# An attention decode kernel: x and bias loads issued after an early square root, and the last values load cut in four instead of three

## The chip, the cores, the metric

One core of one Trainium2 chip. The metric is the device time of one execution in microseconds (us), the median of several. Executions of one kernel mostly agree within about 0.3%. Each run also has its mean *granted clock*: the share of full speed that PE's clock was given, averaged over the execution.

## The reference

Two branches over the same layer-normed x (2 rows of 448) are added to x: attention of 16 heads over the last 4096 positions of a cache with 8 kv heads of 256, and a dense block with a mish activation.

```python
W = min(4096, max(256, Sk // 4))                        # 4096 of 32768 positions
q = (x @ wq)                                            # 2 x 4096
k, v = k_cache[:, :, Sk - W:, :], v_cache[:, :, Sk - W:, :]
p = softmax(einsum("bhqd,bhkd->bhqk", q, k) * Dh ** -0.5)
attn = einsum("bhqk,bhkd->bhqd", p, v) @ wo
h = x @ w1 + b1
dense = (h * tanh(softplus(h))) @ w2
out = x0 + attn + dense                                 # x = layernorm(x0) above
```

Of the 77.66 MB that are read, 67.1 are k and v: 8 heads of 4.19 MB each, twice. Each is read once, so the kernel is a stream with arithmetic beside it.

## The kernel before

All large loads are issued from SP, in the order in which they are used. Only x and the bias are issued from ACT. The beginning:

```python
    x_bf = consts.tile([Bsz, D], BF16)
    nc.scalar.dma_start(out=x_bf[:, :], in_=A_x.flatten_outer_dims())
    b1_sb = consts.tile([1, F], BF16)
    nc.scalar.dma_start(out=b1_sb[:, :], in_=B_b1.rearrange("(o f) -> o f", o=1))
    # ... cut
    for lo, hi in ((0, SC), (SC, NS)):
        nc.sync.dma_start(out=wq_sb[:, lo:hi, :], in_=wq_in[:, lo:hi, :])
    make_identity(nc, ident[:])
    # ... cut
    eps_t = consts.tile([Bsz, 1], FP32)
    nc.vector.memset(eps_t[:], 1e-5)
    stats = consts.tile([Bsz, nc.vector.BN_STATS_DIM], FP32)
    nc.vector.bn_stats(out=stats[:], in_=x_bf[:])
    # ... bn_aggr
    nc.scalar.activation(out=rstd[:], in_=mv[:, 1:2], func=ACT.Sqrt, bias=eps_t[:], scale=1.0)
```

From there one chain leads over xn, its transposes and xs to q (`q_ps`, 28 matmuls with wq) and its transpose, and q is needed for the first scores. The loop over the kv heads, and its end:

```python
    for i in range(Hkv + 1):
        if i + 1 < Hkv:
            load_k(i + 1, (0, T) if i + 1 < Hkv - 1 else (0, T // 2, T))
        if i < Hkv:
            load_v(i, (0, T) if i < Hkv - 1 else (0, T // 2, 7 * T // 8, T))
            load_wo(i, parts=1 if i < Hkv - 1 else 2)
            # ... four pieces of: turn (DVE transpose of k), scores (PE), exp (ACT), turn_p (DVE)
        else:
            close(i - 2)
            carry()              # running sum to the last accumulator: DVE copy, 8 products
        # ... dense block at i == 0
        if i >= 1:
            values(i - 1)        # 32 wide products; the last NFIX = 2 heads: values_fixed,
                                 # 128 small products, in the order of the positions t
        if i == Hkv:
            close(i - 1)         # oT, then 16 products with wo into psA, then out
```

A head's 4096 positions lie as T = 64 on each of 64 partitions per batch row, so the cuts (0, 32, 56, 64) give pieces of 32, 24 and 8 positions, and `values_fixed` makes two products a position: 64, 48 and 16.

The softmax here doesn't subtract the row's maximum and nothing guards it: scores larger than these inputs give would overflow.

## Time and profile before

| | before |
|---|---|
| time, three runs | 190.18 us median (189.81 to 190.29) |
| span of the profiled execution | 188.0 us |
| DMA | 77.66 MB read, 413 GB/s over the span, one queue busy 97.0% |
| PE, DVE, ACT, GpSimd busy | 77%, 57%, 23%, 9% |

Read it from the DMA row: nothing else is busy all the time. The busy slices, the start and the end of the timeline are in the prediction. What is told as a *landing* is from the trace's records of the completions of each of the 16 engines; a load has landed with the last of them.

### The profile page before, as it was taken

Reading aid. Unit: us, or ns where it says so; the run is one execution under the profiler, and the core shown is the slowest. Engines: PE = TensorE matmul, PEld = TensorE weight load, DVE = VectorE, ACT = ScalarE, POOL = GpSimd, SP = SyncE. Lnnn points to the kernel's source line nnn. Section 1 sums busy time; section 2 is a strip of 40 time slices with the busy share of each in tenths; the row PEclk is TensorE's granted clock in tenths of the full one; section 3 lists DMA queues with packets and bytes.
Section 4 is the critical chain, followed back from the end, with each engine's and each line's share of the span. In section 5 each row is a group of like instructions: output and inputs, shape, how many; then the busy total and the mean of one; then the engine's idle time right before and its main releaser. Section 6 shows DMA issues by size and latency. Waiting matters only on the chain.

```text
span 188.0 us, 2346 instructions
## 1 busy us (share of the span) xinstructions
PE 145.5 (77%) x909; PEld 67.0 (36%) x909; DVE 106.8 (57%) x142; ACT 42.5 (23%) x142; POOL 16.5 (9%) x74
## 2 busy tenths in 40 slices
PE   0395089914989988976997599958996689988983
PEld 0131033811334433432442234313442234434662
DVE  6405397049671976079804991099506993977211
ACT  3005015200062124212331223012421242125101
POOL 7000600300003000300030003000030000000000
PEclk9999558855799999997899999975999999999755
DMA  6999899999999999999999999999999899999990
GB/s 220 421 469 446 380 433 442 439 443 439 432 446 418 420 412 421 448 439 386 472 443 441 397 425 446 425 439 422 436 436 439 380 439 429 453 443 387 424 388 35
DMA packets 5652, 77.81 MB, mean 414 GB/s; under 512 B 517, under 2 KB 2569, under 8 KB 2954
## 3 DMA queue, kind: packets, MB, share of 16 engines
q1 hardware_dynamic: 5636, 77.66, 97.0%
q8 instruction: 7, 0.11, 0.2%
q14 instruction: 3, 0.02, 0.0%
q10 hardware_dynamic: 6, 0.01, 0.0%
HBM read 77.67 MB, written 0.00 MB: 413 GB/s over the span
## 4 chain that ended last, share of the span: by engine, by line
DMA 60%; DVE 19%; PE 16%; SPq 2%; ACT 1%; issue 1%; ACTq 0%; DVEq 0%
DMA k<-in_A_k_cache_dram 50%; DVE kt L386 14%; DMA v<-in_A_v_cache_dram 10%; PE o L457 7%; PE sc L398 4%; DVE pT L424 3%; PE psE L210 3%; PE q L507 1%; SPq L362 1%; ACT p L412 1%; SPq L114 0%; PE psA L227 0%; DVE oT L471 0%; PE q L488 0%; SPq L295 0%
## 5 line engine op out<-in xcount | busy, mean ns | idle before, releaser
L386 DVE STREAM_TRANSPOSE kt<-k 128x2048 f32<-128x2048 f32 x32 | 73.1, 2288 | 49.7 <-DMA k<-in_A_k_cache_dram 49.7
L398 PE MATMUL sc<-kt,qdiag 128*128 128x512 bf16 x256 | 63.9, 401 | 17.2 <-DVE kt L386 17.2
L412 ACT ACTIVATE p<-sc,off 128x256 bf16<-128x256 f32 x64 | 33.0, 545 | 73.3 <-PE sc L398 72.6
L398 PEld LDWEIGHTS <-qdiag 128*128 128x128 bf16 x256 | 24.4, 101 | 56.5 <-issue 23.2
L457 PE MATMUL o<-v,pT 128*8 128x512 bf16 x192 | 42.5, 379 | 0.0
L457 PEld LDWEIGHTS <-pT 128*8 128x8 bf16 x192 | 17.2, 92 | 22.4
L424 DVE STREAM_TRANSPOSE pT<-p 128x512 bf16<-128x512 bf16 x32 | 21.7, 677 | 6.1 <-ACT p L412 6.0
L279 POOL COPY qdiag<-qt 32x16 bf16<-32x16 bf16 x64 | 13.0, 249 | 120.9 <-PE sc L398 104.8
L210 PE MATMUL psE<-wo,oT 128*2 128x448 bf16 x28 | 8.6, 444 | 7.2 <-DVE oT L471 7.2
L412 ACT ACTIVATION_READ_ACCUMULATOR p<-sc,off 128x1 f32 x64 | 11.8, 184 | 0.0
L465 ACT COPY o_sb<-o 8x512 f32<-8x512 f32 x6 | 3.5, 575 | 36.3 <-PE o L457 36.3
L210 PE MATMUL psE<-v,act_bf 128*2 128x448 bf16 x14 | 5.2, 567 | 6.5 <-DVE act_bf L344 6.5
L259 PE MATMUL q_ps<-v,xq 128*128 128x512 bf16 x28 | 8.0, 455 | 2.9 <-DMA v<-in_A_wq_dram 2.9
L507 PE MATMUL q<-pT,v 128*128 128x4 bf16 x256 | 7.2, 168 | 0.2 <-DMA v<-in_A_v_cache_dram 0.2
L507 PEld LDWEIGHTS <-v 128*128 128x128 bf16 x256 | 7.3, 102 | 0.3 <-DMA v<-in_A_v_cache_dram 0.3
L269 DVE CAST q_sb<-q_ps 128x512 bf16<-128x512 f32 x2 | 1.3, 687 | 8.6 <-PE q_ps L259 8.6
L259 PEld LDWEIGHTS <-xq 128*128 128x128 bf16 x28 | 3.1, 112 | 7.7 <-issue 3.5
L210 PEld LDWEIGHTS <-oT 128*2 128x2 bf16 x28 | 2.0, 91 | 10.2 <-DVE oT L471 7.8
L210 PEld LDWEIGHTS <-act_bf 128*2 128x2 bf16 x14 | 1.6, 121 | 9.5 <-DVE act_bf L344 6.5
L488 PEld LDWEIGHTS q<-ident_f,o_sb 8*128 8x128 f32 x24 | 3.3, 207 | 3.0 <-issue 3.0
L180 PE MATMUL xnT_ps<-ident,xn_bf 2*128 2x2 bf16 x7 | 0.5, 166 | 4.7 <-DVE xn_bf L138 4.7
L269 ACT CAST q_sb<-q_ps 128x512 bf16<-128x512 f32 x2 | 1.1, 588 | 12.9 <-PE q_ps L259 12.9
(59 smaller groups left out, 46.0 us busy)
## 6 DMA issues: line engine op xcount, KB each, us to landing
k<-in_A_k_cache_dram SPq DMA_DIRECT2D x7, 4096.0 KB, 29.4
v<-in_A_v_cache_dram SPq DMA_DIRECT2D x7, 4096.0 KB, 29.0
k<-in_A_k_cache_dram SPq DMA_DIRECT2D x2, 2048.0 KB, 24.5
v<-in_B_w_dram SPq DMA_DIRECT2D x2, 1568.0 KB, 24.8
wo<-in_A_wo_dram SPq DMA_DIRECT2D x7, 448.0 KB, 29.7
v<-in_A_wq_dram SPq DMA_DIRECT2D x1, 2048.0 KB, 7.7
v<-in_A_v_cache_dram SPq DMA_DIRECT2D x1, 2048.0 KB, 15.4
v<-in_A_wq_dram SPq DMA_DIRECT2D x1, 1536.0 KB, 10.8
```

What stands on the lines that cost most here:

```text
L210: nc.tensor.matmul(psE[:], lhsT=lhsT, rhs=w, start=start, stop=stop, skip_group_check=True)
L259: nc.tensor.matmul(ps[u][:], lhsT=xq[:, s, :, :].rearrange("p j k -> p (j k)"), rhs=wq_sb[:, s, u * N5 : (u + 1) * N5], start=(s == 0), st ...
L269: copy(out=q_sb[:, u * N5 : (u + 1) * N5], in_=ps[u][:])
L279: nc.gpsimd.tensor_copy(out=tv[rows, :, e, j * Q : (j + 1) * Q : HS].rearrange("p n (b h) -> p n b h", b=Bsz), in_=qv[rows, :, h0 : h0 + r ...
L386: nc.vector.transpose(out=kt[:].bitcast(FP32), in_=k[:, half * TH * Dh : (half + 1) * TH * Dh].bitcast(FP32),)
L398: nc.tensor.matmul(psc[:], lhsT=qdiag[i % NW][:, n * NE + e, :], rhs=ktv[:, n, e, :, :], start=(n == 0 and e == 0), stop=(n == NB - 1 and ...
L412: nc.scalar.activation(out=pv[:, b, :, :], in_=sv[:, b, :, :], func=ACT.Exp, scale=scale, bias=off[:, b : b + 1], accum_out=state["rs", i] ...
L424: nc.vector.transpose(out=pT[:], in_=p_t.pop(s)[:])
L457: nc.tensor.matmul(po[:], lhsT=pT_t[i * NH + piece][:, uh * NP * Q : (uh + 1) * NP * Q : HS], rhs=v[:, u * NP : (u + 1) * NP, :].rearrange ...
L465: nc.scalar.copy(out=o_sb[:], in_=po[:])
L488: nc.tensor.transpose(pqv[:, u, c, :], ov[:, u, c, :], ident_f[0:NR, 0:NR])
L507: nc.tensor.matmul(po[:, c, :], lhsT=vv[:, t, c, :], rhs=pTv[:, th, 0:Q:HS], start=(t == 0 and c == 0), stop=(t == T - 1), skip_group_chec ...
```

## The change

Its intent: have ACT fetch the square root's table at the very start by a dummy root, so that the table needn't be fetched when the norm wants it, and let PE start sooner on the last values by cutting their load finer.

```diff
+    eps_t = consts.tile([Bsz, 1], FP32)
+    nc.vector.memset(eps_t[:], 1e-5)
+    root = consts.tile([Bsz, 1], FP32)
+    nc.scalar.activation(out=root[:], in_=eps_t[:], func=ACT.Sqrt)
     x_bf = consts.tile([Bsz, D], BF16)
     nc.scalar.dma_start(out=x_bf[:, :], in_=A_x.flatten_outer_dims())
     ... cut
-    eps_t = consts.tile([Bsz, 1], FP32)
-    nc.vector.memset(eps_t[:], 1e-5)
     ... cut
-            load_v(i, (0, T) if i < Hkv - 1 else (0, T // 2, 7 * T // 8, T))
+            load_v(i, (0, T) if i < Hkv - 1 else (0, T // 2, 13 * T // 16, 15 * T // 16, T))
```

## The prediction

> **What bounds the kernel now.** I read the busy slices first, to see which resource is never idle; then the queue table and the chain of waits; then the timeline of the first 25 us and the last 5 us, where the two edits lie; last the packet and landing records of the transfers there.
>
> ```profile
> DMA  6999899999999999999999999999999899999990
> GB/s 220 421 469 446 380 433 442 439 443 439 432 446 418 420 412 421 448 439 386 472 443 441 397 425 446 425 439 422 436 436 439 380 439 429 453 443 387 424 388 35
> q1 hardware_dynamic: 5636, 77.66, 97.0%
> DMA 60%; DVE 19%; PE 16%; SPq 2%; ACT 1%; issue 1%; ACTq 0%; DVEq 0%
> ```
>
> Between the first and the last slice the DMA engines are busy everywhere: 77.66 MB in a 188.0 us span, 97.0% of it on the one SP queue. The chain names DMA for 60%; its stretches on DVE and PE lie over a queue that is still full. For instance the load of v that is issued at 49.99 us finds the third k load, issued at 31.76, still queued (it landed at 59 to 61 by the landing records); and the last v loads are issued at 163.26 while earlier ones land until 173.9. So about 10 us of transfers lie queued at each of these issues, and a compute stage that slips by less than that starves nothing. The time is then: when the stream starts (first wq row at 1.75 us by the packet records), 77.66 MB at its rate, and the tail after the last byte.
>
> The start, from the timeline:
>
> ```profile
> 0.73 0.55 ACTq L100 DMA_DIRECT2D x_bf<-in_A_x_dram  x1
> 1.31 0.23 ACTq L102 DMA_DIRECT2D b_sb<-in_B_b_dram  x1
> 1.58 1.28 ACT L129 ACT_TABLE_LOAD   x1 [1.58 <-PEq L595]
> 2.06 0.61 DVE L125 BATCH_NORM_STATS2 stats<-x_bf 2x6 f32<-2x448 bf16 x1
> 2.92 0.29 ACT L129 ACTIVATE rstd<-mv,eps_t 2x1 f32<-2x1 f32 x1
> 8.46 8.01 PE L259 MATMUL q_ps<-v,xq 128*128 128x512 bf16 x28 [2.85 <-DMA v<-in_A_wq_dram]
> 21.75 4.50 DVE L386 STREAM_TRANSPOSE kt<-k 128x2048 f32<-128x2048 f32 x2 [3.25 <-DMA k<-in_A_k_cache_dram]
> 24.11 2.29 PE L398 MATMUL sc<-kt,qdiag 128*128 128x512 bf16 x5 [7.65 <-DVE kt L386]
> 40.19 2.31 DVE L386 STREAM_TRANSPOSE kt<-k 128x2048 f32<-128x2048 f32 x1 [7.86 <-DMA k<-in_A_k_cache_dram]
> ```
>
> The table load already lies beside the x load and its statistics: it ends at 2.86, and mv is ready at 2.88 (2.71 + 0.17). The idle times in brackets are the slack: q_ps waited for wq, the first turn 3.25 us for k, and the turn at 40.19 another 7.86 us for the second k load.
>
> The end:
>
> ```profile
> 180.34 1.85 PE L507 MATMUL q<-pT,v 128*128 128x4 bf16 x64
> 182.40 1.87 PE L507 MATMUL q<-pT,v 128*128 128x4 bf16 x64 [0.22 <-DMA v<-in_A_v_cache_dram]
> 184.53 0.58 PE L227 MATMUL psA<-wo,oT 128*2 128x112 bf16 x16 [0.26 <-DVE oT L471]
> ```
>
> Here 64 products of v's first piece run, PE waits 0.22 us for the second, then 64 more run without a gap. By the landing records the last engine's share of v's second piece lands at 182.36, of its third at 183.58, of wo's first half at 184.16, of wo's second half at 184.72. The product with wo's second half is the last 8 of the 16 matmuls at 184.53: at 0.036 us each (0.58/16) it starts at 184.82, only 0.10 us after its data. That is the fact that decides the second edit.
>
> **What the Trainium skill says.** "ScalarE: Activation LUTs", What ACT_TABLE_LOAD costs: about 1283 ns for the load plus a drain. The trace agrees on the load (1.28 us); no separate drain stands in it, as the square root starts 0.06 us after the load. "DMA: Bandwidth & Descriptors", Issuing engines are not separate DMA queues: a load issued from ACT runs on the same 16 engines as one from SP and interleaves with it. The same page, Queues, rings and completion order: an engine serves its queues in turn, a packet at a time. The trace shows what a late comer pays: x was issued at 0.73, its first packet ran at 1.66, 0.93 after the issue and 0.09 before the first wq row. The bias was issued at 1.31, so by the same 0.93 it should have run at 2.24; its one packet ran at 5.43, its completion packet at 6.18, and it landed at 6.49. It sat 3.2 us behind some five wq rows (0.61 us each for 16 KB), and its completion behind one more. That is harmless now, as the bias is first read at 34.05.
>
> **The change part by part.**
>
> 1. Root ahead of the loads. Removed: nothing; the kernel still loads two tables, square root and exp. Added: one ACTIVATE of 2x1 (0.29 us, as rstd's). Moved: the table load to about 0.73, ending at 2.0; the root to about 2.05; the issue of x to between 2.05 and 2.35 (whether ACT waits for the root to end I don't know), against 0.73. x's packets then reach the engines 0.93 later, at 3.0 to 3.3, with wq rows queued ahead, and I let them pay what the bias paid: 3.2 us to the packet, so 6.2 to 6.5, about 0.75 to the completion packet, 0.3 to the landing. x lands at about 7.3 instead of 2.04: 5.3 us later. rstd gains 0.05 us at most from the table being there.
>
> 2. What that does downstream. From x's statistics at 2.06 to the first weight load of q at 7.30 is one chain on DVE, ACT and PE, 5.24 us, all behind x in program order. Shifted by 5.3 it ends at 12.6. wq's second part has landed by 12.03, so q_ps now waits for xq. The 28 matmuls take 8.01 again: they end at 20.6 instead of 16.47, 4.15 later (1.15 was slack). The copies and q's transpose end at 22.65 instead of 18.5. The first turn of k stands behind it on DVE: 22.65 instead of 21.75, 0.9 later. The GpSimd copies, 20.28 + 4.15 = 24.4, still end before that turn (22.65 + 2.3 = 24.95). So the first scores slip by 0.85 and everything up to the turn at 40.19 by the same, where 7.86 us of waiting for k swallows it. The loads that wait for these stages: v's first load, 16.49 to 20.6, while rows queued before it still land until 40.07; k's third, 31.76 to 32.6, likewise. Cost on the path: 0. If x's two packets no longer go ahead of wq, the stream starts up to 0.09 us sooner.
>
> 3. The last values load in four pieces: 32, 20, 8 and 4 positions for 32, 24 and 8. The second piece has 8 rows an engine of 10 KB instead of 12: by 0.611 us for 16 KB, 8 x 2 KB are 0.61 us, so it lands at 181.75. That is before PE has done the first piece (182.19): the 0.22 us wait goes. The third lands halfway between 182.36 and 183.58, at 182.97, the fourth at about 183.6. PE, at 0.029 us a product, would reach the third at 182.19 + 40 x 0.029 = 183.36, the fourth at 183.82, and end at 184.06 instead of 184.27: 0.21 sooner. oT and the first 8 products with wo follow, 184.3 to 184.6. Then wo's second half is needed, and it still lands at 184.72, rather 0.05 later: 8 more packets an engine in the v rows (the records show 159 ns for 4 KB where a quarter of a 16 KB row is 153) and one more completion packet of 9 ns. With 0.05 from landing to start, the last 8 run from 184.77-184.85 to 185.06-185.14; before they ended at 185.11. Gain: 0.0, give or take 0.05. The fourth issue costs SP 0.6 us and delays the issue of wo to 165.8, with 18 us of queue ahead: nothing.
>
> Sum: 0 to -0.09 at the start, 0 in the middle, -0.05 to +0.05 at the end.
>
> **The rivals.**
>
> A. x's delay reaches the stream. For it: x goes from the front of the queue to behind it, and everything hangs on x. Against it: it takes 3.25 + 7.86 us of DVE slack and some 10 us of queue before a transfer starts late. If ACT's packets waited for all of wq and k instead of some five rows, x would land at 21 us (k lands from 20.8 to 21.7), q end at 34, and the first scores near 38; the third k load would be issued near 46, still with queued work until about 50. It would cost 0 to 6 us, 190 to 196. The bias packet speaks against it.
>
> B. The tail gains in full. If wo's second half had landed earlier than I read it, the end would follow PE: 0.21 us, 190.0. And if the fine pieces also slowed the transfers noticeably, the loss might be as much. Either is a tenth of a per cent.
>
> C. The early table is worth its 1.28 us. For it: the load is a visible block before rstd. Against it: it ends 0.02 us before mv is there, and nothing of the start is on the path anyway. It would make 188.9 only if the stream started that much sooner, and SP's issue at 0.73 isn't touched.
>
> D. The pattern of granted clock falls otherwise, as PE starts 4 us later. PE is at half clock in the last 10 us (5 in the last two slices), the products there already at 0.029 us each; a kernel on the transfers moves by a few tenths at most.
>
> **Range and chances.** The middle is 190.18 - 0.05, so 190.1. The three runs of before spread over 0.48 us, and a median of a few runs on another occasion can move by as much; rivals B and D add two tenths; A makes the upper side longer. So 189.6 to 190.7. A 2% move is 3.8 us: on the fast side nothing can pay it, as the bytes don't change; on the slow side only a strong form of A. Hence 0.01, 0.97, 0.02.
>
> **What would show it right or wrong.** Step 1: x issued on ACT near 2.1, bn_stats near 7.3 with an idle time before it that ends on x's DMA; wrong if it starts by 4. Step 2: q_ps from about 12.6 to 20.6, waiting for xq or the weight load, first scores near 24.95, and the turn near 40.2 still waiting for k at an unchanged time. Step 3: no wait on v among the last 128 products, and a wait for wo inside or before the last 16 matmuls, with the out issue within 0.15 us of 185.77. If the DMA line shows a slice below 8 where it had 9, the stream was starved and rival A holds.

## The result, and the profile after

190.28 us median (189.84 to 190.46, 6 runs) against 189.97 (189.70 to 190.29, 6 runs): ratio 1.0014, 95% interval 0.9998 to 1.0030. The same, and inside the range. A ratio here is the mean time of one kernel's fast runs over that of the other's of the same rounds, so it isn't quite the ratio of the medians.

The start, from the timeline of the changed kernel (start and duration in us, engine, line, operation; in brackets the idle time of the engine before it and what ended it):

```profile
0.73 1.28 ACT L102 ACT_TABLE_LOAD   x1 [0.73 <-PEq L597]
0.89 0.54 ACTq L104 DMA_DIRECT2D x_bf<-in_A_x_dram  x1
2.02 0.20 ACT L102 ACTIVATE root<-eps_t 2x1 f32<-2x1 f32 x1
4.56 0.61 DVE L127 BATCH_NORM_STATS2 stats<-x_bf 2x6 f32<-2x448 bf16 x1 [0.52 <-DMA x_bf<-in_A_x_dram]
9.45 8.02 PE L261 MATMUL q_ps<-v,xq 128*128 128x512 bf16 x28 [1.70 <-DVE xq L252]
21.58 4.50 DVE L388 STREAM_TRANSPOSE kt<-k 128x2048 f32<-128x2048 f32 x2 [2.08 <-DMA k<-in_A_k_cache_dram]
40.20 2.31 DVE L388 STREAM_TRANSPOSE kt<-k 128x2048 f32<-128x2048 f32 x1 [8.33 <-DMA k<-in_A_k_cache_dram]
```

ACT issues x at 0.89, *while* the table load runs: only 0.16 later than before. Yet x lands at 4.54, 2.5 us later, and bn_stats starts 2.5 us later. q_ps now waits for xq where it waited for wq, and starts 1.0 later. One row further down nothing of it is left: DVE's first turn still waits for the first k load, and the turn of the second k load starts at 40.20, against 40.19 before.

The end:

```profile
150.19 6.81 PE L400 MATMUL sc<-kt,qdiag 128*128 128x512 bf16 x24
181.29 3.66 PE L509 MATMUL q<-pT,v 128*128 128x4 bf16 x128
185.21 0.54 PE L229 MATMUL psA<-wo,oT 128*2 128x112 bf16 x16 [0.26 <-DVE oT L473]
186.40 0.33 SPq L581 DMA_DIRECT2D out_dram<-res  x1
```

The last 128 products are one row now: no wait for v is left in them. But they begin at 181.29 instead of 180.34 and the output is issued at 186.40 instead of 185.77. PE came late to the end of this execution. The stretches of the changed kernel's profile show where (columns: stretch, its length, busy us and instructions of PE, PEld, DVE, ACT, GpSimd; then the granted PE clock, DMA share, GB/s):

```profile
150.00:160.00 10.00, 10.00 (x41) 4.20 (x41) 6.60 (x5) 3.22 (x12) 0.00 (x0) 0.85 0.99 417
```

and the same stretch of the kernel before:

```profile
150.00:160.00 10.00, 9.39 (x45) 4.17 (x45) 6.54 (x5) 3.23 (x12) 0.00 (x0) 1.00 0.99 421
```

The clock record has a stretch of 3.4 us at half clock from 149.7 to 153.1, in the middle of the scores of one head: 24 matmuls took 6.81 us there. In the profile of before, that stretch of the program ran at full clock (its own half-clock stretches lie elsewhere, 124.8 to 131.6 among them). Whether the change caused this is what the experiments had to say.

### The profile page after: what moved, and what is told of

It reads as the page before. It is cut to its first block, busy times and chain, and to the rows that moved or that the text cites. A ratio compares the mean times of both kernels' runs of the same rounds, so it can differ in the third digit from the quotient of the medians.

```text
span 188.7 us, 2347 instructions
## 1 busy us (share of the span) xinstructions
PE 147.2 (78%) x909; PEld 67.3 (36%) x909; DVE 108.6 (58%) x142; ACT 42.6 (23%) x143; POOL 16.3 (9%) x74
## 4 chain that ended last, share of the span: by engine, by line
DMA 50%; PE 26%; DVE 20%; SPq 1%; ACT 1%; issue 1%; ACTq 0%; DVEq 0%
DMA k<-in_A_k_cache_dram 50%; DVE kt L388 14%; PE sc L400 9%; PE o L459 7%; PE psE L212 4%; PE q L509 4%; DVE pT L426 3%; PE psA L229 1%; PE q L490 1%; ACT p L414 1%; DVE oT L473 1%; PE den L442 0%; SPq L118 0%; DVE osum L494 0%; DVE early L241 0%
## 5 line engine op out<-in xcount | busy, mean ns | idle before, releaser
L400 PE MATMUL sc<-kt,qdiag 128*128 128x512 bf16 x256 | 66.2, 413 | 14.0 <-DVE kt L388 14.0
L400 PEld LDWEIGHTS <-qdiag 128*128 128x128 bf16 x256 | 24.9, 102 | 55.5 <-issue 21.7
L212 PE MATMUL psE<-wo,oT 128*2 128x448 bf16 x28 | 7.9, 411 | 8.2 <-DVE oT L473 8.2
L490 PE MATMUL q<-ident_f,o_sb 8*128 8x8 f32 x24 | 3.8, 264 | 0.0
```

Of the source, the lines that this page charges most:

```text
L212: nc.tensor.matmul(psE[:], lhsT=lhsT, rhs=w, start=start, stop=stop, skip_group_check=True)
L400: nc.tensor.matmul(psc[:], lhsT=qdiag[i % NW][:, n * NE + e, :], rhs=ktv[:, n, e, :, :], start=(n == 0 and e == 0), stop=(n == NB - 1 and ...
L490: nc.tensor.transpose(pqv[:, u, c, :], ov[:, u, c, :], ident_f[0:NR, 0:NR])
```

## The experiments

My theory after the result: the start is swallowed by the waits for k; at the end two chains finish within about a microsecond of each other, the stream (whose last piece is the second half of wo) and PE's own work, and whichever is later in an execution sets the time. The rivals: the late x, or the extra pieces, really cost 0.3 us; or the stream alone sets the end. Eleven kernels ran. All are on record as correct, even `half_v7`, whose result is wrong: the check does not see what it leaves out.

### Each part alone, and the changed kernel again

`front_only` is the changed kernel with the old cuts of v, `tail_only` the kernel before with the new ones:

```diff
 front_only, against the changed kernel
-(0, T // 2, 13 * T // 16, 15 * T // 16, T)
+(0, T // 2, 7 * T // 8, T)
 tail_only, against before
-(0, T // 2, 7 * T // 8, T)
+(0, T // 2, 13 * T // 16, 15 * T // 16, T)
```

> Root and late x alone, v in three pieces. Theory (a late x is swallowed where DVE waits for the second k load at 40.2 us): the same as before within 0.2%, x's load lands near 4.4 us and q_ps starts near 9.45, yet the turn near 40.2 starts within 0.1 us of 40.2. Rival (the late x costs the 0.3 us by which the changed kernel's median is longer): 0.1 to 0.2% over before, and the turn near 40.2 starts later too.

Measured: 190.00 us against 189.95, ratio 1.0003 (0.9991 to 1.0015). x landed at 4.61, q_ps started at 9.52, the turn of the second k load at 40.28. The late x costs nothing that can be measured.

> v in four pieces alone. Theory: no wait on v among the last 128 products, wo's second half lands within 0.15 us of 184.7, and the end is set by that or by PE's own chain: the same as before within 0.2%. Rival 1 (gain in full): 0.2 us less, 0.1%. Rival 2 (the small packets hold up the end): wo's second half lands 0.3 us later or more and the time is 0.15% over before.

Measured: 190.06 us against 189.95, ratio 1.0003 (0.9991 to 1.0015). The end of its timeline:

```profile
180.45 3.89 PE L507 MATMUL q<-pT,v 128*128 128x4 bf16 x128
184.60 0.80 PE L227 MATMUL psA<-wo,oT 128*2 128x112 bf16 x16 [0.26 <-DVE oT L471]
185.04 0.10 PEld L227 LDWEIGHTS <-oT 128*2 128x2 bf16 x7 [0.27 <-issue]
186.05 0.33 SPq L579 DMA_DIRECT2D out_dram<-res  x1
```

This shows the second half of the prediction's third step. No matmul waits for v between two rows any more, but the weight loads still wait 0.18 us for v's last piece (landed at 183.91), so the 128 products end at 184.34, no sooner than before's 184.27. Then wo decides. The 16 products took 0.54 where wo had landed before they began (the first profile of the changed kernel) and take 0.80 here: after the first 9, PE's weight loads stop and go on at 185.04. The view calls the 0.27 "issue", as it names no releaser, but wo's second half landed at 185.00. That landing is 0.3 later than in before's profile, outside the 0.15 that I expected; but `front_only`, with the old pieces, has it at 184.95, so it isn't the small packets.

The changed kernel once more, unedited:

> The changed kernel once more, unedited. Its two parts alone each gave 1.0003 of before, so theory (no part costs anything, and the 1.0014 of the first comparison was where the slow stretches of the clock fell) expects 0.9990 to 1.0012. Rival (the two together cost 0.3 us): 1.0012 to 1.0030, again.

Measured: 189.94 us against 190.05, ratio 0.9999 (0.9986 to 1.0011), as the theory had it; the 1.0014 wasn't repeated. In this profile no half-clock stretch lies between 48 and 178 us, and the end waits for wo as predicted:

```profile
181.84 2.25 PE L509 MATMUL q<-pT,v 128*128 128x4 bf16 x64 [0.34 <-DMA v<-in_A_v_cache_dram]
184.34 0.81 PE L229 MATMUL psA<-wo,oT 128*2 128x112 bf16 x16 [0.26 <-DVE oT L473]
185.80 0.32 SPq L581 DMA_DIRECT2D out_dram<-res  x1
```

PE is early: it begins the last 128 products at 179.59 instead of before's 180.34. So, against the prediction, a wait for v's second piece is left (0.34; the piece landed at 181.79, where it was predicted). PE is done with v at 184.1, and waits inside the 16 products for wo, which landed at 184.75. The output is issued at 185.80, 0.03 from before's 185.77. This is the third step's exchange: the 16 products begin 0.19 sooner than before's (184.34 for 184.53) and end no sooner (185.15 for 185.11).

### Where x's 2.5 us come from

```diff
 root_behind, against front_only: the root moved behind the two loads
-    root = consts.tile([Bsz, 1], FP32)
-    nc.scalar.activation(out=root[:], in_=eps_t[:], func=ACT.Sqrt)
     x_bf = ...; nc.scalar.dma_start(...)
     b1_sb = ...; nc.scalar.dma_start(...)
+    root = consts.tile([Bsz, 1], FP32)
+    nc.scalar.activation(out=root[:], in_=eps_t[:], func=ACT.Sqrt)
```

> The root put behind x and bias on ACT instead of ahead, v in three pieces. Theory (x's late landing comes from its issue missing the moment before the wq rows, by 0.16 us, and not from the table load, as ACT issued x during the load): x's issue is back at 0.73, x lands near 2.0 to 2.5, bn_stats starts by 2.6, and the time is that of before within 0.15%. Rival (the added table load or root itself holds x up): x lands past 3.5.

Measured: 189.97 us against 190.05, ratio 0.9999 (0.9985 to 1.0013).

```profile
0.73 0.55 ACTq L102 DMA_DIRECT2D x_bf<-in_A_x_dram  x1
2.06 2.00 DVE L127 BATCH_NORM_STATS2 stats<-x_bf 2x6 f32<-2x448 bf16 x1
4.31 0.29 ACT L131 ACTIVATE rstd<-mv,eps_t 2x1 f32<-2x1 f32 x1 [1.24 <-DVE mv L129]
```

x is issued at 0.73 and lands at 2.03 again. Its two packets run at 1.66, ahead of the wq rows (the first of these at about 1.75). Issued at 0.89, they run at 2.89 and 3.36 in the changed kernel, among wq rows. So 0.16 us of issue become 2.5 us of landing. This edit moves the table load too (back to 1.58), so alone it doesn't show that x waits for wq rows and not for the load. The packet records speak for the rows: in the five profiles with the late x its packets start anywhere between 2.83 and 3.75, though the table load ends at 2.01 in each; and before's bias waited until 5.43, though its issue was over before the table load began. The bn_stats that takes 2.00 instead of 0.61 is another matter, see the last section.

### How late x may be

```diff
 x_behind_k, against before: x and bias from SP, behind wq and the first k load
-    x_bf = ...; nc.scalar.dma_start(...); b1_sb = ...; nc.scalar.dma_start(...)
     for lo, hi in ((0, SC), (SC, NS)):
         nc.sync.dma_start(out=wq_sb[:, lo:hi, :], in_=wq_in[:, lo:hi, :])
+    k0 = k_pool.tile([P, T * Dh], BF16, tag="k", name="k")
+    nc.sync.dma_start(out=k0[:], in_=src0)      # the first k load, else issued in load_k(0)
+    x_bf = ...; nc.sync.dma_start(...); b1_sb = ...; nc.sync.dma_start(...)
-    load_k(0)
+    k_t[0] = k0
```

> Before, with x and bias issued from SP behind wq and the first k load. x lands near 21.8 instead of 2.04, q_ps ends near 35.5 and the first scores are near 39.8. Theory (queue and slack up to the second k load swallow a late x up to some 10 us): 20 us late is about 8 us more than the 7.9 + 3.3 us of DVE slack, so the turn of the second k load starts near 49 instead of 40.2, and the time is 0 to 4 us over before, most of it won back from idle time later. If x were on the path from the start: 15 us and more over before.

Measured: 193.42 us against 190.11, ratio 1.0184 (1.0159 to 1.0208). The timeline and the stretches:

```profile
21.56 0.61 DVE L128 BATCH_NORM_STATS2 stats<-x_bf 2x6 f32<-2x448 bf16 x1 [19.19 <-DMA x_bf<-in_A_x_dram]
39.13 9.77 PE L401 MATMUL sc<-kt,qdiag 128*128 128x512 bf16 x32 [4.27 <-POOL qdiag L282]
59.50 0.54 SPq L365 DMA_DIRECT2D v<-in_A_v_cache_dram  x1
...
56.00:60.00 4.00, 4.00 (x16) 1.40 (x14) 3.96 (x5) 0.00 (x0) 0.00 (x0) 0.72 0.70 295
60.00:64.00 4.00, 4.00 (x21) 1.76 (x19) 1.92 (x3) 1.94 (x7) 0.00 (x0) 1.00 0.90 336
```

The same two stretches of the kernel before:

```profile
56.00:60.00 4.00, 3.94 (x20) 1.96 (x21) 0.51 (x1) 1.51 (x6) 1.65 (x8) 1.00 1.10 475
60.00:64.00 4.00, 4.00 (x20) 1.71 (x19) 3.57 (x4) 0.00 (x0) 0.00 (x0) 1.00 0.93 401
```

bn_stats 19.5 us late, first scores 15.0 us late, and only 3.3 us in the time. Of the turn's own times I had guessed 49; it started at 47.28, as DVE no longer waited for k anywhere in between. Where most of the 3.3 us arise shows in the stretches: the second v load is issued at 59.50 instead of 49.99, and DMA falls to 295 and 336 GB/s from 475 and 401, because the queue had run down. That is about 1.0 MB less; at the rate of the stretches beside them (some 430 GB/s) I estimate 2.3 us of the 3.0 by which this profile's span is longer. Here a late start cost about the time for which it left the queue short, and not its own 15 to 20 us.

### What the last pieces of v are worth

```diff
 two_pieces, against before
-(0, T // 2, 7 * T // 8, T)
+(0, T // 2, T)
```

> Before, with the last values load in two pieces (32 and 32). By the working of the prediction: the second lands near 183.6, its 64 products end 1.9 us later at 185.5, then oT and the 16 products without a wait for wo: 1.0 to 1.2 us over before, 0.6%. If the end didn't hang on v's pieces: the same.

Measured: 191.01 us against 190.11, ratio 1.0052 (1.0037 to 1.0067).

```profile
183.86 1.87 PE L507 MATMUL q<-pT,v 128*128 128x4 bf16 x64 [1.84 <-DMA v<-in_A_v_cache_dram]
185.99 0.54 PE L227 MATMUL psA<-wo,oT 128*2 128x112 bf16 x16 [0.26 <-DVE oT L471]
```

PE waits 1.84 for the second piece and the 16 products start at 185.99, after wo has long landed (184.94). So going from two pieces to three is worth 0.9 us, a little under the 1.0 to 1.2 expected; going from three to four is worth nothing, as the next thing to land is already the later one.

### Taking work off the stream, and off PE

```diff
 half_v7, against before: WRONG RESULT ON PURPOSE
-(0, T // 2, 7 * T // 8, T)
+(0, T // 2)
-                    lhsT=vv[:, t, c, :],
+                    lhsT=vv[:, t % (T // 2) if i == Hkv - 1 else t, c, :],
```

> WRONG RESULT ON PURPOSE: of the last values load only the first half is loaded (2.1 MB less), and its second half's products read the first half again. Theory (PE's chain is as long as the transfers): at most 0.4 us less than before, though 2.1 MB at 420 GB/s are 5.0 us. Rival (the transfers alone set the end): 4 to 5 us less.

Measured: 188.90 us (188.38 to 190.03, 6 runs) against 189.95, ratio 0.9954 (0.9927 to 0.9981).

```profile
184.10 0.54 PE L227 MATMUL psA<-wo,oT 128*2 128x112 bf16 x16 [0.26 <-DVE oT L471]
```

Both expectations were off, mine by half a microsecond and the rival by three or more. 2.1 MB less bring 0.9 us, not 5: PE's chain stands right behind the stream. In this profile all of wo had landed at 179.81, and yet the last 16 products start at 184.10, only 0.43 sooner than before's. And the runs now spread over 1.65 us with the granted clock: the three at a mean clock of 0.923 to 0.931 took 188.38 to 188.64, the three at 0.869 to 0.890 took 189.16 to 190.03. So I read PE's chain as ending between 0 and some 1.5 us ahead of the stream, by where its slow stretches fall.

Before's own runs show a weaker order of the same kind. Of the 33 that ran beside the experiments, the 18 at a mean clock of up to 0.890 have a median of 190.12, the 15 at 0.895 and more one of 189.80. (It is weakest in the first eleven, where the fastest, 189.71, had 0.878.) The stream doesn't hold them all: where the clock was low, PE ends later in some.

The third last head's values done as 128 small products, 3.5 us on PE in place of 7.0:

```diff
 after_fix3, against the changed kernel, and before_fix3, against before
-    NFIX = 2
+    NFIX = 3
```

> The changed kernel with the third last group of values also done the other way round (128 small products, about 3.5 us on PE, in place of 32 wide ones, 7.0 us). Theory (in the last 42 us PE's chain and the transfers end within some tenths of each other, and in the changed kernel's profile PE was the later): the last 128 products wait for v's pieces, wo's second half is waited for or lands less than 0.1 us ahead, the time is 0.3 to 0.6 us under the changed kernel and 0 to 0.3 under before. Rival (the transfers alone set the end): the same as the changed kernel within 0.1 us. Rival (PE's chain alone): some 3 us less.

Measured: 190.91 us (190.14 to 191.18) against 189.95, ratio 1.0053 (1.0040 to 1.0066). It is slower than both kernels, which neither theory nor rival had. Its profile, of the fastest of its runs:

```profile
172.75 3.57 PE L509 MATMUL q<-pT,v 128*128 128x4 bf16 x128 [1.02 <-DMA v<-in_A_v_cache_dram]
179.87 4.09 PE L509 MATMUL q<-pT,v 128*128 128x4 bf16 x122
184.31 0.32 PE L509 MATMUL q<-pT,v 128*128 128x4 bf16 x6 [0.36 <-issue]
```

PE's gain is spent waiting 1.02 us for the last head but one's v, so the end begins at 179.87: sooner than in the changed kernel's first profile (181.29), but no sooner than in its second (179.59). Then there is a stop of 0.36 before the last six products, of which the profile names no cause. The other runs of this kernel are 0.3 to 1.0 us slower than the profiled one; what they lost isn't in view here.

> Before, with the third last group of values done as 128 small products too. In the changed kernel this cost 0.6 us instead of gaining 0.3 to 0.6. If it is a cost of the small products themselves (PE in the last 30 us), before loses as much: 0.3 to 0.6% over before. If it only met the changed kernel's fourth piece: within 0.15% of before.

Measured: 190.48 us against 190.05, ratio 1.0027 (1.0014 to 1.0040).

```profile
182.43 1.71 PE L507 MATMUL q<-pT,v 128*128 128x4 bf16 x58 [0.68 <-DMA v<-in_A_v_cache_dram]
184.62 0.32 PE L507 MATMUL q<-pT,v 128*128 128x4 bf16 x6 [0.48 <-issue]
```

That is 0.27%, between the two answers that I had foreseen. The stop is there without the fourth piece too: 0.48, before the last six, though all of v had landed at 183.63. So it comes with the small products. But the loss against before is 0.4 to 0.5 us here and about 1.0 there, so a share of the fourth piece isn't ruled out. What stops PE stays open. A candidate that no run tests is a wait for instructions: both stops come before the same PE instruction, and in both the next 16 KB packet of the profile's instruction queue starts 1.10 us after PE goes on (185.41 and 185.72).

### The same end with PE out of the way

```diff
 late_carry, against the changed kernel; late_carry3: the same against before
     # in values_fixed, in the loop over t
+            if i == Hkv - 1 and t == T // 2:
+                carry()
     # in the loop over the heads
             close(i - 2)
-            carry()
```

> The changed kernel with carry() (the running sum's copy to the last accumulator, on PE a wait of 0.7 us and 8 products) moved from before v's last 128 products into their middle, where the changed kernel has slack on v's second piece. Theory (after its first 0.2 us of gain the end is held by PE's chain where the granted clock made it late, and otherwise by wo's second half): the first 64 of the 128 start 1 to 1.4 us sooner, the median is 0.1 to 0.5 us under the changed kernel's 190.28, and the last 8 products with wo start within 0.15 us of its second half's landing. Rival (PE's lateness is not what holds the end): the same as the changed kernel.

Measured: 189.88 us (189.72 to 189.95) against 190.11, ratio 0.9990 (0.9977 to 1.0003).

```profile
180.03 1.90 PE L511 MATMUL q<-pT,v 128*128 128x4 bf16 x64
181.86 0.55 PE L229 MATMUL psA<-early,ident_f 2*2 2x112 f32 x8
182.35 1.92 PE L511 MATMUL q<-pT,v 128*128 128x4 bf16 x64
184.53 0.67 PE L229 MATMUL psA<-wo,oT 128*2 128x112 bf16 x16 [0.26 <-DVE oT L473]
185.85 0.33 SPq L582 DMA_DIRECT2D out_dram<-res  x1
```

This profile has its half-clock stretch at the same place as the first profile of the changed kernel (149.8 to 153.2; there 149.7 to 153.1), and PE reaches the end equally late (in both the last head but one's products with wo start at 178.00). Yet the output is issued at 185.85 instead of 186.40, and the 16 products take 0.67, waiting again for wo, which landed at 184.80. It is the only edit whose runs all stay below 190.

Sorted by clock, the runs say more than the medians do. At a mean clock of up to 0.890 the four runs of `late_carry` took 189.72 to 189.90, the six of before in the same rounds 190.11 to 190.34. At 0.895 and more it is 189.87 and 189.95 against 189.74 to 189.94. So the move gains some 0.4 us where the clock was low and nothing where it was high, as the theory has it: in the first case PE's lateness holds the end, in the second the landing of wo. The comparison was made afterwards and the runs are few, but in the first case the two groups don't overlap.

> The same move in the kernel before (v in three pieces). Theory: PE waits about 0.3 to 1 us for v's second piece instead of 0.22, and the time is within 0.2 us of before, since wo's second half was already the later one in its profile; four pieces (late_carry) are 0 to 0.3 us better than this. Rival (PE holds the end): 0.5 us or more under before.

Measured: 189.90 us (189.70 to 190.14) against 190.11, ratio 0.9993 (0.9980 to 1.0006). As expected within 0.2 us of before, and four pieces gain nothing measurable over three here either. I had expected a wait of 0.3 to 1 us for v's second piece: it was 0.15, as PE again had a slow stretch near 150 (149.7 to 153.1). So had `before_fix3` (150.4 to 153.8). Neither has the root or the fourth piece, so the change isn't needed for such a stretch. late_carry and late_carry3 have the lowest medians of their rounds, by 0.2 us, but both intervals include no difference; I don't call them faster.

## Why the prediction was right

**The sum, right.** "0 to -0.09 at the start, 0 in the middle, -0.05 to +0.05 at the end": measured 1.0014 and 0.9999 in two comparisons, and 1.0003 for each part alone, all with intervals that include no difference.

**Step 1, right in kind, its size too large.** The step supposed that ACT issues x between 2.05 and 2.35, after the table load or the root. ACT issued it at 0.89, during the load. The second term, 3.2 us behind wq rows as the bias paid, was too large as well: by the prediction's 0.93 x should have run at 1.82, and it ran at 2.89 and 3.36, 1.1 to 1.5 later. That is about one wq row and not five: the rows that began by 2.1 us took 0.92 to 1.57 each. (The packet records name no engine, so this is read from the times.) So x landed at 4.54 for a predicted 7.3. The mechanism, that a small load which comes after the wq rows must wait among them, agrees with `root_behind` (0.16 us of issue for 2.5 us of landing) and with the packet records. The outlook's test "wrong if it starts by 4" came out at 4.56, so only just.

**Step 2, right.** The slip was 1.0 at q_ps instead of 4.15, and swallowed one wait earlier than I thought: at the first k load already (first turn at 21.58, still waiting). The turn at 40.2 didn't move, in any of the five profiles with the late x that I read there. Rival A, "0 to 6 us" for x at 21, measured 3.3 with x at 21.5, by the starved queue that it named. One reading was a little off, without effect: the third k load landed at 58.5 to 60.3, not 59 to 61.

**Step 3, right on the loads, with one thing left out on PE's side.** v's second, third and fourth pieces landed at 181.78, 183.02 and 183.68 (predicted 181.75, 182.97, 183.6), wo's second half at 184.76 (184.72, rather 0.05 later). In the second profile of the changed kernel the finer pieces let PE be done with v 0.18 sooner than before's (184.09 for 184.27), and that was given back in a wait for wo inside the last 16 products, which took 0.81. But a wait of 0.34 for v was left, as PE came early. In `tail_only` the wait for wo came too (0.80), without a gain ahead of it. In the first profile of the changed kernel there was no wait for v and none for wo, as PE came late. Left out was that PE doesn't always reach this end at the same time, so that it is the later chain in some executions. "The out issue within 0.15 us of 185.77" failed in the first profile (186.40) and held in the second (185.80). Rival D had it as "a few tenths at most"; a half-clock stretch in the last 42 us made it 0.6 in that one profile. Over the runs it was tenths: 0.3 between the medians of before's runs at low and at high clock.

**Rival C, right to reject.** `front_only` has the table at 0.73 and the same time. No run has both an early table and an early x (in `root_behind` the load is at 1.58, as before); that this would gain nothing either rests on the slack at the start.

Open: why PE stops before the last six products with NFIX = 3; and whether the first comparison's 0.3 us was the clock alone. Its interval included no difference and the repetition gave none. Five of the changed kernel's six runs there had a mean clock of 0.868 to 0.889 and took 190.21 to 190.46; the sixth had 0.929 and took 189.84. The clocks of before's runs in that comparison aren't on record.

## What to carry to other kernels

In a kernel that streams all the time, ask of a part at the start only whether it lets the queue run empty, and of a part at the end only which of the last landings and the last compute comes last: finer pieces of one load gain up to the next landing and no further. When two chains end within a microsecond, one profile shows which was later that time, not which is the bound; repeat it, or take work off each in turn. A small load that others hang on is best issued ahead of the large ones, as 0.16 us at the issue was 2.5 us at the landing; here the slack hid it.

## What the Trainium skill lacked or had wrong

- "ScalarE: Activation LUTs", What ACT_TABLE_LOAD costs: it gives about 1283 ns for the load plus a drain of about 1380 ns. The load took 1.28 us in every profile, but no drain was to be seen: the root started 0.01 us after it (0.73 + 1.28, then 2.02). The section doesn't say that ACT goes on issuing DMAs during the load; here x was issued 0.16 us after its start.
- "DMA: Bandwidth & Descriptors", Queues, rings and completion order: it says that an engine takes its queues in turn, a packet at a time. The runs give the price: x's packets of 896 bytes, issued 0.16 us later, ran 1.2 to 2.1 us later among rows of 16 KB (five profiles), and the bias's packet ran at 5.43 for an issue at 1.31.
- "TensorE: Matmul & The Clock Gate", Part 1, puts half clock down to idle windows of about 3.4 us, and names short idle times too, without a figure for them. Here half clock came without any wholly idle window: from 146.3 to 149.7 PE was busy for 1.74 of 3.4 us in the first profile of the changed kernel, idle for at most 1.66 at a stretch, and half clock followed to 153.1. In the second profile PE was busy for 1.75 in the same stretch, and full clock followed. That one stretch cost 0.9 us on PE (178.00 for 177.04).
- "GPSIMD Engine Reference", Key points, says that GpSimd shares its SBUF interfaces with VectorE, for certain forms of instruction. None of the pages tells which length an instruction gets when the starts on both engines agree to 0.01 us. GpSimd filled tiles from 1.25 to 4.0 us; a DVE cast of 32x32 that starts at 1.34 took 1.03 us in some profiles (`late_carry`) and 2.71 in others (the changed kernel), where it ends with the last fill. bn_stats took 2.00 for 0.61 in `root_behind`, begun before such a cast had ended. That GpSimd is the cause is argued, not tested.
